# One row of small products per token tile, transposes apart, and a written order for TensorE in the last stage of a linear-attention kernel

## The chip, the cores and the metric

The kernel runs on one core of a Trainium2 chip. The core has five engines, each with its own queue of instructions that it works off in order: TensorE (PE in the profile; its weight loads are PEld), VectorE (DVE), ScalarE (ACT), GpSimd (POOL) and SyncE (SP), which here issues the transfers. [...] TensorE writes into PSUM, a small memory that DVE and ACT empty into the main on-chip memory, SBUF; transfers move data between SBUF and the memory outside (HBM). The metric is the device time of one execution in microseconds (us), the median of several runs.

## The reference

The input x has 2048 tokens of 1024 numbers. Two branches read its normalized form:

```python
xn = _layernorm(x)
# branch A: linear attention, 32 heads of 32
q, k, v = split(xn @ wqkv)
phi_q = concat([softmax(q @ w_phi), softmax(-(q @ w_phi))])     # per head, 64 features
phi_k = the same of k
kv = einsum("sf,sd->fd", phi_k, v);  z = sum_s phi_k            # per head
o  = (phi_q @ kv) / (phi_q @ z + 1e-6)
s  = o @ wo
# branch B: gated feed-forward, 1024 -> 3584 -> 1024
g  = silu( (silu(xn @ w1) * (xn @ w3)) @ w2 )
out = x + s * g
```

All numbers are 32-bit floats. The large products are made of three passes over a number split in a high and a low part.

## The kernel before

The kernel goes through stages: normalization, keys and values, the feed-forward branch, and last the queries with the attention output. The large products of the earlier stages are done by a Strassen-like scheme of seven products in place of eight; those stages are the same in both kernels. What the change touches is the last stage, which goes through the 16 token tiles of 128 tokens each.

For one token tile the last stage does this:

- `load_q` brings the tile of xn, `split_q` splits it into high and low parts (`xh`; a cast on ACT, line 92, and a subtraction on DVE, line 93).
- `project_q(xT, c)` makes half c of the tile's queries, already multiplied by w_phi: `project`, line 101, 24 matmuls of 128x128 by 512 columns, into a PSUM tile `pm` (tag "mm", three buffers).
- `queries(p, c)` turns that half into normalized features `e`: maxima, minima and two subtractions on DVE (lines 1000 to 1003), Exp on ACT (1006), a product with z, `ez`, on POOL (1007), two sums (1011 over e, 1015 over ez), a chain of small operations (1013 to 1020) and the last multiply (1021) on DVE.
- `attend(c, e)` is the small work on TensorE: e is transposed in two quarters of four 128x128 blocks (line 1146, PSUM tile `pt2`, three buffers), each copied to SBUF by ACT (`et`, line 1148), and multiplied by the per-head kv matrices `kvu` (line 1152): products with 64 rows and 32 columns of weights and 128 moving columns, 16 for each half, into the PSUM tile `po` of two banks, one buffer. A cast and a subtraction (`split`) make `oT` of it, high and low.
- `finish(i, oT)` multiplies oT by wo in two halves of 24 matmuls (`project`), multiplies by the gate g and adds x (`gx`), and stores.

The loop is skewed by one tile: while the queries of tile i are made, the features of tile i-1 are attended and finished. The first tile's features, `es[0]` and `es[1]`, are made at the end of the stage before: es[1] while the last but one round of that stage runs, es[0] in the last one.

The order of instructions on each engine is set by a scheduler that ranks by program order and its own cost model, wherever the program does not say otherwise. `in_order(engines)` opens a stretch in which the named engines keep the written order exactly; `in_order()` ends it. Before, the last stage has SP alone in written order, and only for the first iteration; TensorE's order is the scheduler's. It put the second row of small products, which needs `po` free again, among the matmuls of `project_q(xT, 1)`, and two of the second half's transposes ahead of the first row.

Of the kernel before, what the change touches and what calls it, by code (L numbers as in the profile page):

```python
# [8 lines left out]
F = mybir.dt.float32  # L9
# [8 lines left out]
P = 128  # L18
NT = S // P
# [10 lines left out]
def tile_kernel(ctx: ExitStack, tc: tile.TileContext, x, wkT, wqT, wv, wphi, wo, w1, w3, w2, out):  # L30
    nc = tc.nc
    open_pools = {}

    def pool(name, bufs, **kw):

        open_pools[name] = tc.tile_pool(name=name, bufs=bufs, reuse_waits="tile", **kw)
        return open_pools[name].__enter__()
# [5 lines left out]
    ENG = mybir.EngineType  # L43
# [3 lines left out]
    def in_order(*engines):  # L47

        if ordered:
            ordered.pop().__exit__(None, None, None)  # L50
        if engines:
            ordered.append(tc.manual_schedule(engines=set(engines)))
            ordered[0].__enter__()
# [18 lines left out]
    g_d = [dram.tile([P, D], F, name=f"g_d{i}") for i in range(NT)]  # L72
# [17 lines left out]
    def split(hi, lo, src, by=None):  # L90

        nc.scalar.copy(hi, src)  # L92
        (by or nc.vector).tensor_sub(lo, src, hi.bitcast(F))  # L93

    def project(ps, xT, w, tag="mm"):

        p = ps.tile([P, 512], F, name="pm", tag=tag, bufs=3 if tag == "mm" else BANKS["a"])
        n = 0
        for dch in range(ND):
            for a, b in PASSES:  # L100
                nc.tensor.matmul(p, xT[dch][:, a], w(dch, b), start=n == 0, stop=n == 3 * ND - 1)  # L101
                n += 1
        return p
# [34 lines left out]
    work = pool("work", 5)  # L138
# [5 lines left out]
    ps = pool("ps2", 2, space=PSUM)  # L144
# [25 lines left out]
    def quad(name, dt=R):  # L170
        return qp.tile([P, 2, 4, P], dt, name=name, tag="q")
# [7 lines left out]
    ident = misc.tile([P, P], F, name="ident")  # L179
# [134 lines left out]
    for j in range(4):  # L314
        sl = slice(32 * j, 32 * j + 32)
# [599 lines left out]
    ps = pool("ps", 2, space=PSUM)  # L915
    BANKS = {"a": 2, "b": 3, "c": 2}
    pend = None
    ready = []
    for c in range(2):
# [4 lines left out]
        for i in range(len(pairs)):  # L924
            nxt, end = {}, i + 1 == len(pairs)

            def steps():
                for j in range(7):
                    if j == 0:
                        if i + 2 == len(pairs) and c == 0:  # L930
                            for m in range(2):
                                wbn.update(fetch(3, m))
                        if not (end and c):
                            nxt.update(reload((i + 1) % len(pairs)))
                        if c and 0 < i < 5:
                            load_b(0, i - 1)

                    if end and c == 0 and j in (0, 1, 4, 5, 6):
                        wbn.update(fetch(3, {0: 2, 1: 3}.get(j, j)))
                    if end and c and j in (1, 4):  # L940
                        ready.append(a_first(0, 0) if j == 1 else a_second(*ready[0]))
                    yield

            pend = heads(i, xo, wb, steps(), pend)
# [5 lines left out]
    accp = pool("acc", 1)  # L950
# [13 lines left out]
    wq, wos, es = {}, {}, {}  # L964
# [15 lines left out]
    def load_q(i):  # L980
        two = quad("xf", F)
        for hf in range(2):
            nc.sync.dma_start(two[:, hf], xn_d[:, 4 * hf:4 * hf + 4, i * P:(i + 1) * P])
        return [two[:, hf] for hf in range(2)]

    def split_q(xf):
        xT = []
        for t in xf:
            xh = quad("xh")
            split(xh[:, 0], xh[:, 1], t)  # L990
            xT += [xh[:, :, k] for k in range(4)]
        return xT

    def queries(p, c):

        e = accp.tile([P, 16, 2, DH], F, name="e", tag="accE", bufs=3)
        ez = accp.tile([P, 2 * 512], F, name="ez", tag="accZ", bufs=3)
        mm = small.tile([P, 2, 16], F, name="mm2")
        p3 = p.rearrange("p (h f) -> p h f", f=DH)
        nc.vector.tensor_reduce(mm[:, 0, :], p3, axis=AX.X, op=OP.max)  # L1000
        nc.vector.tensor_reduce(mm[:, 1, :], p3, axis=AX.X, op=OP.min)
        nc.vector.tensor_sub(e[:, :, 0], p3, mm[:, 0, :].unsqueeze(2).to_broadcast([P, 16, DH]))
        nc.vector.tensor_sub(e[:, :, 1], mm[:, 1, :].unsqueeze(2).to_broadcast([P, 16, DH]), p3)
        ef = e.rearrange("p h s f -> p (h s f)")
        e3 = e.rearrange("p h s f -> p (h s) f")
        nc.scalar.activation(ef, ef, AF.Exp)
        nc.gpsimd.tensor_mul(ez, ef, zb[c])
        sums = small.tile([P, 2, 16, 2], F, name="sums")
        by = small.tile([P, 16, 2], F, name="by")
        t = small.tile([P, 2, 16], F, name="rho")  # L1010
        nc.vector.tensor_reduce(sums[:, 0].rearrange("p h s -> p (h s)"), e3, axis=AX.X, op=OP.add)

        nc.vector.reciprocal(t[:, 0], sums[:, 0, :, 1])
        nc.vector.tensor_mul(t[:, 0], sums[:, 0, :, 0], t[:, 0])
        nc.vector.tensor_reduce(sums[:, 1].rearrange("p h s -> p (h s)"), ez.rearrange("p (h f) -> p h f", f=DH),
                                axis=AX.X, op=OP.add)
        nc.vector.tensor_mul(t[:, 1], sums[:, 1, :, 1], t[:, 0])
        nc.vector.tensor_add(t[:, 1], t[:, 1], sums[:, 1, :, 0])
        nc.vector.reciprocal(by[:, :, 0], t[:, 1])
        nc.vector.tensor_mul(by[:, :, 1], by[:, :, 0], t[:, 0])  # L1020
        nc.vector.tensor_mul(e3, e3, by.rearrange("p h s -> p (h s)").unsqueeze(2).to_broadcast([P, H, DH]))
        return ef

    def project_q(xT, c, tag="mm"):
        return project(ps, xT, lambda k, a: wq[c, k][:, a], tag)
# [31 lines left out]
    for r, new in enumerate(steps):  # L1057
        kb, i = new or (NKB, 0)
# [5 lines left out]
        if new is None:  # L1064
            in_order(ENG.SP, ENG.Activation, ENG.DVE, ENG.Pool)
            xT = split_q(xf)
# [33 lines left out]
        if end:  # L1100
# [12 lines left out]
            if i == 4:  # L1113
                xf = load_q(0)
            elif i == 5:
                xT = split_q(xf)
            elif i > 5:
                if i == 6:

                    kvu = work.tile([P, 2, G, DH], F, name="kvu", tag="h1", bufs=2)  # L1120
                    for a in range(2):
                        for h in range(2):
                            sl = slice(64 * a + 32 * h, 64 * a + 32 * h + 32)
# [3 lines left out]
            if i == 7:  # L1127
                xf = load_q(1)
# [4 lines left out]
    ps = pool("ps4", 3, space=PSUM)  # L1133
    gate(*pairs[-1])
    for k in range(14, 16):
        load_wo(k, accp.tile([P, 2, 512], R, name="wos", tag="accW", bufs=2))
    in_order(ENG.SP)

    def attend(c, e):


        po = ps.tile([P, 2, 512], F, name="po", tag="po", bufs=1)
        for q in range(2):
            pt = ps.tile([P, 4, P], F, name="pt2", tag="tr", bufs=3)
            for g in range(4):
                nc.tensor.transpose(pt[:, g, :], e[:, (4 * q + g) * P:(4 * q + g + 1) * P], ident)  # L1146
            et = work.tile([P, 4, P], F, name="et", tag="w")
            nc.scalar.copy(et, pt)
            for g in range(4):
                for hh in range(2):  # L1150
                    sl = slice(64 * hh, 64 * hh + 64)
                    nc.tensor.matmul(po[32 * g:32 * g + 32, hh, q * P:(q + 1) * P], kvu[sl, g % 2, 4 * c + 2 * q + g // 2], et[sl, g],  # L1152
                                     start=True, stop=True, skip_group_check=True)
        oT = quad("oT")
        o4 = oT.rearrange("p u (h q) t -> p u h q t", q=2)
        split(o4[:, 0], o4[:, 1], po[:, :, :2 * P].rearrange("p h (q t) -> p h q t", t=P))
        return oT

    def finish(i, oT):
        for c in range(2):  # L1160
            cs = slice(c * 512, c * 512 + 512)
            gx = accp.tile([P, 2, 512], F, name="gx", tag="accZ", bufs=3)
            nc.sync.dma_start(gx[:, 0], g_d[i][:, cs])
            nc.sync.dma_start(gx[:, 1], x[i * P:(i + 1) * P, cs])
            p = project(ps, [t[:, :, k] for t in oT for k in range(4)], lambda k, a: wos[c, k][:, a])
            nc.vector.tensor_mul(gx[:, 0], p, gx[:, 0])
            (nc.vector if i + 1 == NT else nc.gpsimd).tensor_add(gx[:, 0], gx[:, 0], gx[:, 1])
            nc.sync.dma_start(out[i * P:(i + 1) * P, cs], gx[:, 0])

    pend = 0, es[0], es[1]  # L1170
    for i in range(1, NT):
        if i < NT - 1:
            xf = load_q(i + 1)
        e0 = queries(project_q(xT, 0), 0)
        oT = [attend(0, pend[1]), attend(1, pend[2])]
        p = project_q(xT, 1)
        if i + 1 < NT:
            xT = split_q(xf)
        e1 = queries(p, 1)
        finish(pend[0], oT)  # L1180
        pend = (i, e0, e1)
        if i == 1:
            in_order()
    finish(pend[0], [attend(0, pend[1]), attend(1, pend[2])])
    close("ps4", "rb", "acc", "q", "work", "small", "misc", "ra", "rw", "edge_r", "edge_l")


# [36 lines left out]
```

## Time and profile before

| | |
|---|---|
| time, median of 3 runs | 2427.62 us (2425.49 to 2428.64) |
| the profiled execution | 2427.67 us, of which the profile's span is 2425.9 us |
| TensorE busy | 2394.2 us, 99% of the span |
| DVE, ACT, POOL busy | 73%, 36%, 8% |
| last stage | from about 2020 us to the end |

A profile line of the timeline gives the start in us from the span's start, the time from the first start to the last end, the engine, the line of the kernel, the operation, the tile written and those read, shapes, and the count of instructions in the group. In brackets stands the idle time just before, and what ended it. TensorE's instructions overlap, so the distance between the starts of two groups tells more than the duration of one. Rows of windows give, for each stretch, the busy time and count of PE, PEld, DVE, ACT and POOL, then the granted TensorE clock as a share of full speed, and the transfers. The small products appear twice in the profile for each one in the program.

### The profile page before, as it was taken

The numbers are of one execution on the slowest core, as the hardware profiler recorded it, in microseconds if no ns is written. First come the engines' busy times: TensorE is split into PE (matmuls) and PEld (weight loads), VectorE is DVE, ScalarE is ACT, GpSimd is POOL, SyncE is SP. The second block draws the span as 40 slices with busy tenths as digits, with TensorE's granted clock in tenths as the row PEclk, the third lists the DMA queues.
The fourth block names the chain that finished last, engine by engine and source line by source line (L and its number), as shares of the span: only waits on it lengthen the run. The fifth ranks groups of instructions, "written<-read, shape, count | busy, mean of one in ns | idle before, by whom it ended". The sixth has DMA issues, their size and how long they took to land.

```text
span 2425.9 us, 35682 instructions
## 1 busy us (share of the span) xinstructions
PE 2394.2 (99%) x13650; PEld 1965.1 (81%) x13650; DVE 1773.2 (73%) x2883; ACT 880.4 (36%) x1549; POOL 196.4 (8%) x162
## 2 busy tenths in 40 slices
PE   6999999999999999999999999999999999999999
PEld 5888888888888888888787888888888887777777
DVE  7877787875688878764565666678878777777775
ACT  5545454443355444442111114322222244222221
POOL 2000000000000000000000000011111112222322
PEclk9999999999999999999999999999999999999999
DMA  8456799997788886666958745442445476222222
GB/s 280 141 193 226 261 337 341 319 321 221 254 296 296 311 281 239 238 219 240 339 175 345 249 157 200 175 163 89 157 174 182 157 255 231 73 89 86 70 88 70
DMA packets 295274, 517.86 MB, mean 213 GB/s; under 512 B 19904, under 2 KB 168128, under 8 KB 293312
## 3 DMA queue, kind: packets, MB, share of 16 engines
q1 hardware_dynamic: 295104, 515.59, 61.6%
q8 instruction: 107, 1.75, 0.3%
q14 instruction: 63, 0.52, 0.1%
HBM read 329.65 MB, written 185.87 MB: 213 GB/s over the span
## 4 chain that ended last, share of the span: by engine, by line
PE 95%; DMA 1%; DVE 1%; ACT 1%; SPq 0%; issue 0%; ACTq 0%; DVEq 0%
PE bankb L613 24%; PE pm L101 14%; PE bankb L1038 13%; PE bankc L613 12%; PE bankb L806 7%; PE bankc L1038 6%; PE banka L613 6%; PE bankc L806 3%; PE banka L1038 3%; PE banka L806 2%; PE po L1152 1%; PE pw L250 1%; PE pkv L791 1%; PE pt L1146 1%; DMA op2T<-wkv_d0T 1%; PE pt L218 1%
## 5 line engine op out<-in xcount | busy, mean ns | idle before, releaser
L93 DVE TENSOR_TENSOR bo<-rw,bo 128x512 fp32r<-128x512 f32 x336 | 230.4, 688 | 158.7 <-ACT bo L92 156.0
L92 ACT CAST bo<-rw 128x512 fp32r<-128x512 f32 x336 | 206.3, 618 | 5.5 <-DMA xo_d1S<-xoS 3.4
L1038 PE MATMUL bankb<-bo,as 128*128 128x512 f32 x816 | 200.9, 389 | 0.0
L101 PE MATMUL pm<-wq,xh 128*128 128x512 f32 x768 | 185.8, 394 | 0.0
L1038 PEld LDWEIGHTS bankb<-bo,as 128*128 128x128 f32 x816 | 153.2, 188 | 31.8
L101 PEld LDWEIGHTS pm<-wq,xh 128*128 128x128 f32 x768 | 141.9, 188 | 31.7 <-issue 3.0
L613 PE MATMUL bankb<-op0S,bo 128*128 128x512 f32 x672 | 162.9, 391 | 0.9 <-ACT op0S L92 0.5
L613 PE MATMUL bankc<-op0S,bo 128*128 128x512 f32 x672 | 162.4, 391 | 0.0
L613 PE MATMUL bankc<-op1S,bo 128*128 128x512 f32 x672 | 161.2, 389 | 0.0
L613 PE MATMUL bankb<-op1S,bo 128*128 128x512 f32 x672 | 161.2, 389 | 0.0
L613 PE MATMUL bankb<-op0A,bo 128*128 128x512 f32 x672 | 159.7, 391 | 0.6 <-DVE bo L93 0.3
L613 PE MATMUL bankb<-op1A,bo 128*128 128x512 f32 x672 | 157.5, 389 | 0.1
L613 PEld LDWEIGHTS bankb<-op1A,bo 128*128 128x128 f32 x672 | 126.0, 188 | 27.1 <-DVE u L655 0.9
L613 PEld LDWEIGHTS bankb<-op0S,bo 128*128 128x128 f32 x672 | 125.2, 188 | 27.5 <-ACT op0S L92 0.9
L613 PEld LDWEIGHTS bankb<-op1S,bo 128*128 128x128 f32 x672 | 126.1, 188 | 26.2
L613 PEld LDWEIGHTS bankc<-op1S,bo 128*128 128x128 f32 x672 | 126.1, 188 | 26.2
L613 PEld LDWEIGHTS bankb<-op0A,bo 128*128 128x128 f32 x672 | 125.1, 188 | 26.8 <-DVE bo L93 0.6
L613 PEld LDWEIGHTS bankc<-op0S,bo 128*128 128x128 f32 x672 | 125.3, 188 | 25.9 <-DVE op0S L93 0.3
L1038 PE MATMUL bankc<-bo,as 128*128 128x512 f32 x576 | 146.2, 389 | 0.0
L101 PE MATMUL pm<-wos,oT 128*128 128x512 f32 x576 | 136.2, 389 | 0.0
L101 PEld LDWEIGHTS pm<-wos,oT 128*128 128x128 f32 x576 | 108.0, 188 | 22.7 <-issue 0.2
L1038 PEld LDWEIGHTS bankc<-bo,as 128*128 128x128 f32 x576 | 108.1, 188 | 22.5
(234 smaller groups left out, 4249.3 us busy)
## 6 DMA issues: line engine op xcount, KB each, us to landing
rw<-in_w SPq DMA_DIRECT2D x112, 512.0 KB, 4.5
hr<-h_d SPq DMA_DIRECT2D x56, 512.0 KB, 3.5
h_d<-h SPq DMA_DIRECT2D x111, 256.0 KB, 5.1
xoS<-xo_d0S SPq DMA_DIRECT2D x32, 512.0 KB, 8.4
xoS<-xo_d1S SPq DMA_DIRECT2D x32, 512.0 KB, 3.6
room<-in_w SPq DMA_DIRECT2D x56, 256.0 KB, 5.9
xoA<-xo_d0A SPq DMA_DIRECT2D x24, 512.0 KB, 7.8
xoA<-xo_d1A SPq DMA_DIRECT2D x24, 512.0 KB, 3.6
```

The costliest lines, as they stand in the source:

```text
L92: nc.scalar.copy(hi, src)
L93: (by or nc.vector).tensor_sub(lo, src, hi.bitcast(F))
L101: nc.tensor.matmul(p, xT[dch][:, a], w(dch, b), start=n == 0, stop=n == 3 * ND - 1)
L218: nc.tensor.transpose(pt[:, k, :], half[:, k * P:(k + 1) * P], ident)
L250: nc.tensor.matmul(pw[:, g, :], wr[:, g], bd[:, 4 * c + g, :], start=True, stop=True)
L613: nc.tensor.matmul(bank[b], bos[tb, f][bn][:, w, k], ao[an][:, u, k], start=first and n == 0, stop=LAST[b] == an and n == 11, skip_group_c ...
L791: nc.tensor.matmul(pkv[sl, m], e[:, m // 4, (m % 4) * P + 32 * h:(m % 4) * P + 32 * h + 32], v[:, 4 * (m % 4) + h], start=first and m == 0 ...
L806: nc.tensor.matmul(bank[b], xo[an][:, u, k], wb[bn][:, w, k], start=an in ("A11", "A12", "S1") and n == 0, stop=LAST[b] == an and n == 11, ...
L1038: nc.tensor.matmul(bank[b], t[:, u, pos + k], bos[kb, bn, k][:, w], start=first and n == 0, stop=LAST[b] == an and n == 5, skip_group_chec ...
L1146: nc.tensor.transpose(pt[:, g, :], e[:, (4 * q + g) * P:(4 * q + g + 1) * P], ident)
L1152: nc.tensor.matmul(po[32 * g:32 * g + 32, hh, q * P:(q + 1) * P], kvu[sl, g % 2, 4 * c + 2 * q + g // 2], et[sl, g], start=True, stop=True ...
```

## The change

Three things are changed in the last stage.

- `turn_e` does the transposes and copies of one quarter of a feature half; `attend` takes four such copies and issues all 32 small products in one row, into one `po` tile of [128, 2, 4, 128], the same two banks with both halves side by side. The casts and subtractions for both halves of oT follow it.
- `finish` does one of its two halves, c, at a time. The transposes of the first half of the next features (`e0`) stand between the two halves; those of the second half (`e1`) stand right ahead of the row of small products. For the first tile, the transposes of `es[0]` stand ahead of the loop.
- TensorE is in written order in the whole of the last stage, with SP beside it until the end of the first iteration.

The written order on TensorE in one iteration is so: the first query projection, eight transposes, 32 small products, the second query projection, half of the output projection, eight transposes, the other half. In the built program the other engines' order moves too: on DVE the first subtraction into oT now stands behind the sum over ez and the reciprocal (before: ahead of the sum over e), the second one four small operations later; on ACT the two casts into oT stand together behind the Exp, and the copies of the transposes of e0 behind the Exp of e1. The number of instructions of each kind is the same.

```diff
-    in_order(ENG.SP)
-
-    def attend(c, e):
-        po = ps.tile([P, 2, 512], F, name="po", tag="po", bufs=1)
-        for q in range(2):
-            pt = ps.tile([P, 4, P], F, name="pt2", tag="tr", bufs=3)
-            for g in range(4):
-                nc.tensor.transpose(pt[:, g, :], e[:, (4 * q + g) * P:(4 * q + g + 1) * P], ident)
-            et = work.tile([P, 4, P], F, name="et", tag="w")
-            nc.scalar.copy(et, pt)
+    in_order(ENG.SP, ENG.PE)
+
+    def turn_e(e, q):
+        pt = ps.tile([P, 4, P], F, name="pt2", tag="tr", bufs=3)
+        for g in range(4):
+            nc.tensor.transpose(pt[:, g, :], e[:, (4 * q + g) * P:(4 * q + g + 1) * P], ident)
+        et = work.tile([P, 4, P], F, name="et", tag="w")
+        nc.scalar.copy(et, pt)
+        return et
+
+    def attend(ets):
+        po = ps.tile([P, 2, 4, P], F, name="po", tag="po", bufs=1)
+        for k, et in enumerate(ets):
             for g in range(4):
                 for hh in range(2):
                     sl = slice(64 * hh, 64 * hh + 64)
-                    nc.tensor.matmul(po[32 * g:32 * g + 32, hh, q * P:(q + 1) * P], kvu[sl, g % 2, 4 * c + 2 * q + g // 2], et[sl, g],
+                    nc.tensor.matmul(po[32 * g:32 * g + 32, hh, k], kvu[sl, g % 2, 2 * k + g // 2], et[sl, g],
                                      start=True, stop=True, skip_group_check=True)
-        oT = quad("oT")
-        o4 = oT.rearrange("p u (h q) t -> p u h q t", q=2)
-        split(o4[:, 0], o4[:, 1], po[:, :, :2 * P].rearrange("p h (q t) -> p h q t", t=P))
+        oT = []
+        for c in range(2):
+            o = quad("oT")
+            o4 = o.rearrange("p u (h q) t -> p u h q t", q=2)
+            split(o4[:, 0], o4[:, 1], po[:, :, 2 * c:2 * c + 2])
+            oT.append(o)
         return oT
...
-    def finish(i, oT):
-        for c in range(2):
-            cs = slice(c * 512, c * 512 + 512)
+    def finish(i, oT, c):
+        cs = slice(c * 512, c * 512 + 512)
...
-    pend = 0, es[0], es[1]
-    for i in range(1, NT):
+    ets, e1 = [turn_e(es[0], q) for q in range(2)], es[1]
+    for i in range(1, NT + 1):
         if i < NT - 1:
             xf = load_q(i + 1)
-        e0 = queries(project_q(xT, 0), 0)
-        oT = [attend(0, pend[1]), attend(1, pend[2])]
-        p = project_q(xT, 1)
-        if i + 1 < NT:
-            xT = split_q(xf)
-        e1 = queries(p, 1)
-        finish(pend[0], oT)
-        pend = (i, e0, e1)
+        if i < NT:
+            e0 = queries(project_q(xT, 0), 0)
+        ets += [turn_e(e1, q) for q in range(2)]
+        oT = attend(ets)
+        if i < NT:
+            p = project_q(xT, 1)
+            if i + 1 < NT:
+                xT = split_q(xf)
+            e1 = queries(p, 1)
+        finish(i - 1, oT, 0)
+        if i < NT:
+            ets = [turn_e(e0, q) for q in range(2)]
+        finish(i - 1, oT, 1)
         if i == 1:
-            in_order()
-    finish(pend[0], [attend(0, pend[1]), attend(1, pend[2])])
+            in_order(ENG.PE)
+    in_order()
```

More of the change, by code (lines that the diff above doesn't have):

```diff
@@ L1157, in attend @@
-        return oT
-    def finish(i, oT):
-        for c in range(2):
-            cs = slice(c * 512, c * 512 + 512)
[L1162 to L1168, printed above, removed]
@@ L1170, in tile_kernel @@
-    pend = 0, es[0], es[1]
-    for i in range(1, NT):
+        oT = []
[4 more added lines that the diff above has]
+            oT.append(o)
+        return oT
+    def finish(i, oT, c):
+        cs = slice(c * 512, c * 512 + 512)
+        gx = accp.tile([P, 2, 512], F, name="gx", tag="accZ", bufs=3)
+        nc.sync.dma_start(gx[:, 0], g_d[i][:, cs])
+        nc.sync.dma_start(gx[:, 1], x[i * P:(i + 1) * P, cs])
+        p = project(ps, [t[:, :, k] for t in oT for k in range(4)], lambda k, a: wos[c, k][:, a])
+        nc.vector.tensor_mul(gx[:, 0], p, gx[:, 0])
+        (nc.vector if i + 1 == NT else nc.gpsimd).tensor_add(gx[:, 0], gx[:, 0], gx[:, 1])
+        nc.sync.dma_start(out[i * P:(i + 1) * P, cs], gx[:, 0])
```

## The prediction

> **What bounds the kernel.** I read the page's engine table first, then PE's timeline of one token tile, then the other engines around it, then both ends of the last stage.
>
> ```profile
> PE 2394.2 (99%) x13650; PEld 1965.1 (81%) x13650; DVE 1773.2 (73%) x2883; ACT 880.4 (36%) x1549; POOL 196.4 (8%) x162
> ```
>
> TensorE is busy 99% of the span, so time goes only where PE works less, and comes only where PE waits. The stage the change touches runs from about 2020 us to the end. One token tile of it, PE's timeline (start, us, then the group):
>
> ```profile
> 2154.41 1.25 PE L1146 MATMUL pt<-ident,e 128*128 128x128 f32 x10
> 2155.74 0.94 PE L1152 MATMUL po<-et,kvu 64*32 64x128 f32 x32
> 2156.61 0.88 PE L1146 MATMUL pt<-ident,e 128*128 128x128 f32 x6
> 2157.24 1.84 PE L101 MATMUL pm<-wq,xh 128*128 128x512 f32 x7
> 2159.02 0.78 PE L1152 MATMUL po<-et,kvu 64*32 64x128 f32 x32
> 2159.72 4.19 PE L101 MATMUL pm<-wq,xh 128*128 128x512 f32 x17
> 2163.75 5.60 PE L101 MATMUL pm<-wos,oT 128*128 128x512 f32 x24
> ```
>
> I call the two query projections P0 and P1, the two output projections F0 and F1 (24 matmuls each), the transposes T and the small products S (each of the kernel's 32 is two instructions here, so 64). t0 is the moment a tile's P0 has issued; here 2154.41. From starts of groups: ten T take 1.33 up to S, six take 0.63 (0.105 each); S in two halves takes 0.87 and 0.70; the seven matmuls before the second S take 1.78 and the 17 after it 4.03. No wait of PE is printed in this tile. The start of the stage and later starts of T:
>
> ```profile
> 2020.23 5.60 PE L101 MATMUL pm<-wq,xh 128*128 128x512 f32 x24
> 2025.67 1.25 PE L1146 MATMUL pt<-ident,e 128*128 128x128 f32 x10
> ...
> 2077.45 1.25 PE L1146 MATMUL pt<-ident,e 128*128 128x128 f32 x10
> ...
> 2385.41 1.25 PE L1146 MATMUL pt<-ident,e 128*128 128x128 f32 x10
> ```
>
> P0's 24 matmuls take 2025.67 - 2020.23 = 5.44, 0.227 each; so the seven and the 17 above took 0.19 and 0.17 more than their number asks for, and a change between wide and small products costs about that each time, four times a tile. The starts of T are t0 of tiles 1, 3 and 15: the first two periods together are 51.78, the other twelve 307.96 / 12 = 25.66 each. 96 wide matmuls are 21.77 of that; 3.89 are T, S and changes.
>
> **The change: steady tiles.** Removed: one of the two small rows' entries and exits. 16 T stay at 0.109 = 1.74. One row of 64: entered at 0.24 (1.33 - 10 x 0.109), body and exit 0.70 plus two more sixteens at 0.33 (half of the 0.65 that a 32 would add), 1.35; re-entry of the wide ones 0.17. Sum 3.50 against 3.89: 0.39 less, period 25.27. Bounds for the row: twice 0.70 (no saving inside) and 2 x 0.50 + 0.20 = 1.20; I take the middle, since both halves show the same spacing. Now the covers in written order, with DVE and ACT of the same tile:
>
> ```profile
> 2155.10 1.07 ACT L1148 COPY et<-pt 128x512 f32<-128x512 f32 x2 [11.20 <-PE pt L1146]
> 2154.61 0.69 DVE L1000 TENSOR_REDUCE mm<-pm 128x16 f32<-128x512 f32 x1 [2.40 <-PE pm L101]
> ...
> 2165.94 0.68 DVE L1000 TENSOR_REDUCE mm<-pm 128x16 f32<-128x512 f32 x1
> ...
> 2173.42 0.63 DVE L1166 TENSOR_TENSOR gx<-pm,gx 128x512 f32<-128x512 f32 x1
> ...
> 2395.99 0.68 DVE L1000 TENSOR_REDUCE mm<-pm 128x16 f32<-128x512 f32 x1
> ...
> 2406.10 1.22 DVE L1021 TENSOR_TENSOR e<-e,by 128x1024 f32<-128x1024 f32 x1
> ```
>
> The row's first 32 instructions use copies made in the tile before; the last 32 need copies of T issued just ahead. Those copies end at t0 + 0.69 + 0.59 and + 1.76, and S reaches them at about t0 + 1.76 and 2.06: covered by S itself, without reserve to speak of; if ACT were late, PE waits as long. The copies of the other half (mid-F) queue behind the second Exp on ACT, but are needed only after t0 of the next tile, over 8 us on.
>
> The new wait is at F0. One PSUM tile means that the casts and the subtractions into oT come after all of S, and in the new DVE order the first oT subtraction stands behind the sum over ez, where before it stood ahead of the sum over e. The second query chain of this tile shows the length of that queue undisturbed: from its first reduce (2165.94) to the instruction behind the reciprocal (2173.42) 7.48, which itself takes 0.63. The first chain starts at t0 + 0.20, so oT's low half is ready at t0 + 8.31, and PE starts 0.15 to 0.2 later: 8.50. PE comes there by its own work at 0.87 (eight T) + 0.24 + 1.35 + 0.17 + 5.44 = 8.07, and the first matmul with the low half is the third, 8.52. The two are level. If PE's part were shorter than reckoned, DVE's 8.50 would hold and nothing more would be won, so 0.39 a tile is also about the most; if the queue is longer by x, each tile is longer by x. DVE's work has room: the second chain starts at 11.53 before, and some 0.7 later after, since subtractions that lay in a wait now lie ahead of it; from its start to the writing of e it takes 11.33 (2395.99 to 2407.32), and one multiply more ends it at about t0 + 24.2, below 25.27. The first e is written about 0.6 ahead of the second chain's start, 11.6, and T asks for it at t0 + 13.5. SP's loads of gx and xf stand behind the stores that wait for POOL's add, and shift with it by about 1 us against several us until they are used. These I cost at nothing.
>
> The first two tiles differ:
>
> ```profile
> 2045.56 0.63 DVE L1166 TENSOR_TENSOR gx<-pm,gx 128x512 f32<-128x512 f32 x1
> ...
> 2051.55 0.69 DVE L1166 TENSOR_TENSOR gx<-pm,gx 128x512 f32<-128x512 f32 x1 [2.14 <-PE pm L101]
> ```
>
> In the first iteration SP is in written order, the second gx is loaded after the first out is stored, and 5.99 us lie between the two multiplies (the page blames PE; what came last there was the load). This is unchanged, so the first chain of tile 2 starts 0.8 late, and where oT and F0 are level F0 now waits for it. I take 0.15 of gain for tiles 1 and 2 together. Tiles 1 to 14: -0.15 - 12 x 0.39 = -4.83.
>
> **The change: the start.** In written order the first instructions of the stage are the eight T of es[0], and PE can issue nothing past them; before, P0 of tile 1 went first and hid them. es[0] is the last thing that the stage before made:
>
> ```profile
> 2023.75 1.23 DVE L1021 TENSOR_TENSOR e<-e,by 128x1024 f32<-128x1024 f32 x1
> ```
>
> It is written at 2024.98. DVE's order ahead of it is the same in both kernels, and the PE work it hangs on was issued by 2020.23. PE needs about 0.15 behind such a write (2406.10 + 1.22 to the row of 2407.47, below): T starts at 2025.13, P0 at 2026.00, and t0 of tile 1 is 2031.44 instead of 2025.67: +5.77, of which 4.9 is an idle PE. Queued behind T are P0, all of tile 1, and with it every engine.
>
> A PE that idles for 4.9 us may come back slow. What this trace shows:
>
> ```profile
> 14.55 3.75 PE L250 MATMUL pw<-bd,room_b 128*128 128x128 f32 x16 [14.55 <-DMA room_b<-in_wkT]
> 18.10 4.58 PE L218 MATMUL pt<-ident,xt 128*128 128x128 f32 x28
> 24.59 0.66 PE L218 MATMUL pt<-ident,xt 128*128 128x128 f32 x4 [1.90 <-ACT xf L223]
> ...
> 31.51 1.95 PE L250 MATMUL pw<-bd,room_b 128*128 128x128 f32 x16
> ...
> 2420.30:2423.70 3.40, 0.94 (x5) 0.44 (x3) 1.38 (x2) 0.00 (x0) 0.00 (x0) 1.00 0.02 8
> 2423.70:2425.90 2.20, 0.00 (x0) 0.00 (x0) 0.00 (x0) 0.00 (x0) 0.00 (x0) 0.50 0.28 106
> ```
>
> After 14.55 us of nothing, sixteen products took 3.75 us, later 1.95: half speed. The 28 transposes behind them took 4.58 where 0.109 each would be 3.2 with the last one's end; some 13 of them were slow too, so half speed lasted about 6.2 us into the work. After 1.9 us of idle four transposes took the normal time. At the end the granted clock is 0.50 some 2.5 us after the last matmul (2418.36 + 2.88). So 4.9 us idle is past the point. 6.2 us at half speed lose 0.47 of it, 2.9, on the one restart in the trace; ends 0 (no drop) and 3.3 (7 us); I take 2.5, nearest to the restart, a little under it because PE works densely from the first.
>
> [...]
>
> **The change: the end.**
>
> ```profile
> 2407.47 0.41 PE L1146 MATMUL pt<-ident,e 128*128 128x128 f32 x2 [0.80 <-ACT et L1148]
> ...
> 2408.59 0.59 ACT L92 CAST oT<-po 128x512 fp32r<-128x512 f32 x1 [1.19 <-PE po L1152]
> 2418.36 2.88 PE L101 MATMUL pm<-wos,oT 128*128 128x512 f32 x12
> ```
>
> Before, PE's last issue slot ends at 2418.36 + 12 x 0.227 = 2421.08, t0 + 35.67 of tile 15. After, F1 ends at about t0 + 19.8, and the last T needs the second e of tile 15: its chain started at t0 + 10.58 before, starts 0.5 later behind two oT subtractions, and lasts 11.33: T at t0 + 22.55, after 2.7 of idle. Then po is done 0.87 + 0.24 + 1.43 = 2.54 later (0.78 for a row of 32, 0.65 for 32 more), the cast follows by 0.1 (an estimate) and takes 0.59, F0 starts at + 3.3 and its third matmul, behind the subtraction, at + 4.04; 46 wide ones are 10.43: end at t0 + 37.0. That is +1.3. Here the cover of S's results is gone (no P1 is left), while before half of them lay under F0's first matmuls. 2.7 us of idle lie between the 1.9 that did nothing and the 4.9; whether the clock halves again is open, at the price of the start. I take 1.5, half of 2.9; ends 0 and 3.3.
>
> **Sum.** +5.77 + 2.5 - 4.83 + 1.3 + 1.5 = +6.2. The profiled execution took 2427.67 (its span 2425.9 and 1.8 around it), the median of the runs 2427.62, so nothing is to be moved: 2433.8, +0.25%. A measurement of this kernel can tell about 0.2%, 4.9 us, from no change.
>
> **Rivals.** (1) The clock drops at the start alone: 2433.8 - 1.5 = 2432.3, about on the bound of 0.2%. For it: 2.7 us is short. (2) It drops nowhere: 2.5 less again, 2429.8. For it: the row at 24.59; against it the 0.50 at the end. (3) The first T does not wait, because es[0] is written before PE gets there; then T only moves, start term +0.87, no first drop, 2427.67 + 0.87 - 4.83 + 1.3 = 2425.0, or up to 2428 with a drop at the end: not slower. It decides if e is written before 2020.2; the row at 2023.75 is against it. (4) DVE's queue ahead of oT grows by 0.3 us or more a tile (POOL's product late, ACT's Exp behind a copy): 14 x 0.3 = 4.2 more, 2438. Nothing in the rows shows such a delay, but PE in written order would meet every one. (5) The one row saves nothing, small products costing by number alone: 4.8 more, 2438.6; the 0.17 to 0.24 per change speak against it.
>
> **Numbers.** Forecast 0.42, (1) 0.25, (2) 0.12, (3) 0.06, (4) and (5) together 0.15. The range reaches from (2) to (4): 2429 to 2438.5. The forecast's own range, with the clock terms' ends, is 2431.5 to 2436. Slower by over 0.2%: nine tenths of the forecast, half of (1), all of (4) and (5), 0.65; faster by over 0.2% only if (3) comes with a larger gain per tile, 0.04; the rest 0.31.
>
> **What would show it.** On PE's timeline: an idle of 4.9 before the first transposes of the stage, put down to DVE's e, and groups of 128x128 at double spacing behind it, with a granted clock under 1.0 in that slice; periods of 25.2 to 25.3 in tiles 3 to 14, one row of 64 small products; small waits at the third matmul of F0 on DVE's oT; 2.7 of idle before the last eight transposes. Wrong would be: no idle at 2020, or periods above 25.5 or below 25.1.

## The result, and the profile after

| | before | changed |
|---|---|---|
| time, median | 2427.42 us (2425.49 to 2429.3, 11 runs) | 2433.46 us (2432.37 to 2434.9, 11 runs) |
| the profiled execution's span | 2425.9 us | 2432.5 us |

The ratio is 1.0026, 95% interval 1.0017 to 1.0035: slower by 6.0 us, where 2433.8 was forecast. Both profiles have nearly the same busy time of TensorE (2394.2 and 2395.2 us); the difference is waiting and clock. The start of the last stage, from the timeline of TensorE of the changed kernel, with DVE's line for the features that it waits for (start, us, engine, line, operation, tiles, shapes, count, and in brackets the idle before and what ended it):

```profile
2018.68 1.52 PE L1038 MATMUL bankb<-bo,as 128*128 128x512 f32 x6
2023.56 1.23 DVE L1021 TENSOR_TENSOR e<-e,by 128x1024 f32<-128x1024 f32 x1
2024.93 1.94 PE L1144 MATMUL pt<-ident,e 128*128 128x128 f32 x8 [4.73 <-DVE e L1021]
2026.53 7.27 PE L101 MATMUL pm<-wq,xh 128*128 128x512 f32 x24
2033.64 1.03 PE L1144 MATMUL pt<-ident,e 128*128 128x128 f32 x8
2034.60 1.30 PE L1155 MATMUL po<-et,kvu 64*32 64x128 f32 x64
2035.84 5.73 PE L101 MATMUL pm<-wq,xh 128*128 128x512 f32 x24
2041.41 0.62 PE L101 MATMUL pm<-wos,oT 128*128 128x512 f32 x2
2043.22 5.29 PE L101 MATMUL pm<-wos,oT 128*128 128x512 f32 x22 [1.20 <-DVE oT L93]
```

TensorE stands for 4.73 us until DVE has written the features of the first tile. What comes then is slow: eight transposes in 1.94 us where the next eight take 1.03, and 24 wide matmuls in 7.27 where 5.6 is usual. The views of windows show the granted clock (the number before the last two):

```profile
2024.40:2027.70 3.30, 2.77 (x11) 2.61 (x12) 0.39 (x1) 1.17 (x2) 0.00 (x0) 0.50 1.01 376
...
2031.20:2034.50 3.30, 3.30 (x20) 2.73 (x18) 0.66 (x2) 0.17 (x1) 0.00 (x0) 1.00 0.94 274
...
2412.00:2416.00 4.00, 3.65 (x72) 2.88 (x72) 0.41 (x1) 1.40 (x3) 1.27 (x1) 0.57 0.73 235
```

By the trace's record of the granted clock it is halved from 2022.98 to 2029.80 us, that is 2.0 us before the first wait ends and for 4.87 us of the work behind it, and once more near the end, from 2412.10 to 2415.51. A steady tile and the end, TensorE's timeline again, with DVE's first subtraction into oT in the steady tile:

```profile
2085.97 1.04 PE L1144 MATMUL pt<-ident,e 128*128 128x128 f32 x8
2086.94 1.30 PE L1155 MATMUL po<-et,kvu 64*32 64x128 f32 x64
2088.18 5.73 PE L101 MATMUL pm<-wq,xh 128*128 128x512 f32 x24
2093.68 0.63 DVE L93 TENSOR_TENSOR oT<-po,oT 128x512 fp32r<-128x512 f32 x1
2093.75 5.90 PE L101 MATMUL pm<-wos,oT 128*128 128x512 f32 x24
2099.49 1.03 PE L1144 MATMUL pt<-ident,e 128*128 128x128 f32 x8
...
2389.55 1.04 PE L1144 MATMUL pt<-ident,e 128*128 128x128 f32 x8
...
2406.68 2.88 PE L101 MATMUL pm<-wos,oT 128*128 128x512 f32 x12
2411.96 1.82 PE L1144 MATMUL pt<-ident,e 128*128 128x128 f32 x8 [2.40 <-DVE e L1021]
2413.71 1.95 PE L1155 MATMUL po<-et,kvu 64*32 64x128 f32 x64
2416.41 6.01 PE L101 MATMUL pm<-wos,oT 128*128 128x512 f32 x24 [0.76 <-ACT oT L92]
...
2424.97 2.88 PE L101 MATMUL pm<-wos,oT 128*128 128x512 f32 x12
```

From tile 3 (2085.97) to tile 15 (2389.55) a period is 303.58 / 12 = 25.30 us, 0.36 less than before. All 64 small products stand in one row, as written. The first output projection takes 2099.49 - 2093.75 = 5.74 from start to the next start where 24 matmuls without a wait take 5.44: it waits 0.30 for that subtraction. The whole, by the marks of the prediction (the starts of the transposes in tiles 1, 3 and 15):

| stretch | before | changed | difference |
|---|---|---|---|
| to the first transposes of tile 1 | 2025.67 | 2033.64 | +7.97 |
| tiles 1 and 2 | 51.78 | 52.33 | +0.55 |
| tiles 3 to 14 | 307.96 | 303.58 | -4.38 |
| tile 15 to TensorE's last issue (last group + 12 x 0.227) | 35.67 | 38.14 | +2.47 |

The sum is +6.61, the difference of the two spans.

### The profile page after: what moved, and what is told of

The parts are those of the page before. It is cut to its first block, busy times and chain, and to the rows that moved or that the text cites. A ratio compares the mean times of both kernels' runs of the same rounds, so it can differ in the third digit from the quotient of the medians.

```text
span 2432.5 us, 35683 instructions
## 1 busy us (share of the span) xinstructions
PE 2395.2 (98%) x13650; PEld 1971.2 (81%) x13650; DVE 1772.6 (73%) x2883; ACT 880.1 (36%) x1549; POOL 196.5 (8%) x162
```

## The experiments

Each kernel ran beside the kernel before on the same chip. "Time" is the median; the ratio is to the kernel before. The runs e1 to e4, e5 to e8, and e9 with e10 form three groups, in which the kernel before took 2426.63, 2427.17 and 2427.01 us (2427.42 beside the changed kernel). So a difference between runs of two groups is uncertain by nearly 1 us, and where it matters it is also given against the kernel before of the same group.

| run | time, us | ratio, 95% interval |
|---|---|---|
| e1, first transposes behind the first projection | 2425.96 | 0.9996 (0.9988 to 1.0005) |
| e2, last tile in halves | 2432.61 | 1.0024 (1.0014 to 1.0034) |
| e3, both | 2424.51 | 0.9991 (0.9983 to 1.0) |
| e4, both, and the oT subtraction earlier | 2419.42 | 0.9968 (0.9956 to 0.9981) |
| e5, the first wait filled with work | 2430.75 | 1.0015 (1.0006 to 1.0023) |
| e6, both waits filled | 2430.38 | 1.0012 (1.0004 to 1.0021) |
| e7, the kernel before in written order | 2576.85 | 1.0615 (1.06 to 1.0629) |
| e8, as e4 with two rows of small products | 2425.37 | 0.9992 (0.9983 to 1.0001) |
| e9, one row, the scheduler's order | 2428.0 | 1.0005 (0.9996 to 1.0014) |
| e10, as e4 without the last tile in halves | 2418.86 | 0.9966 (0.9954 to 0.9979) |

The theory: the start costs a wait and a halved clock, the end the same on a smaller scale, and the tiles gain up to a ceiling set by DVE's queue. The first rival: the loss is spread over the stage by the written order. The second: the written order, not the one row, brings the gain.

**e1: the place of the first transposes.**

```diff
-    ets, e1 = [turn_e(es[0], q) for q in range(2)], es[1]
+    ets, e1 = None, es[1]
     for i in range(1, NT + 1):
...
             e0 = queries(project_q(xT, 0), 0)
+        if i == 1:
+            ets = [turn_e(es[0], q) for q in range(2)]
```

> The changed kernel with one thing moved: the eight transposes of es[0] stand behind the first query projection of the stage, directly ahead of those of es[1], where before they stood ahead of it. Theory (the start costs 4.7 us of idle TensorE and about 2.5 us of half clock, and the tiles gain): the first row of small products starts about 7.3 us earlier, no idle of more than 1 us near 2020, time about 2426.2, tile periods unchanged at 25.30. Rival (the loss is spread over the stage by the written order, and the wait at the start only shifts work that would wait elsewhere): time stays at 2432 to 2434.

2425.96 us, 7.5 less than the changed kernel (6.7 against the kernel before of each). TensorE's timeline of this run:

```profile
2018.80 5.61 PE L101 MATMUL pm<-wq,xh 128*128 128x512 f32 x24
2024.25 1.93 PE L1144 MATMUL pt<-ident,e 128*128 128x128 f32 x16
```

No wait is left ahead of the transposes; the projection covers the time until the features are there. From the end of the stage before (2020.04 in the changed kernel, 2018.80 here) to the first row of small products it is 14.56 us in the changed kernel and 7.31 here (that row starts at 2026.11), 7.3 less as expected. So the start's term is shown, with its size, and the rival of a spread loss falls.

**e2 and e3: the last tile in halves.**

```diff
+    p = bank()
+    part(p, oT[0], 1, 0)
+    po = ps.tile([P, 2, 4, P], F, name="po", tag="po", bufs=1)
+    o = half(po, 0, ets)
+    part(p, oT[1], 1, 1)
...
+    for c in range(2):
+        part(ends[c], o, c, 0)
+    ets = [turn_e(e1, q) for q in range(2)]
+    o = half(po, 1, ets)
+    for c in range(2):
+        part(ends[c], o, c, 1)
```

`half` issues 32 of the small products and makes one half of oT; `part` issues the 12 output matmuls that need that half.

> The changed kernel with another last tile: the small products of its first half go between the two halves of the last but one tile's second output projection, the output products that need only this half come next, and the transposes of the second half, its small products and the rest of the output products come last. Theory (the end costs 2.4 us, by an idle of 2.4 us before the last transposes, the half clock behind it and 0.8 us before the last output products): about 2431.1, no wait above 2 us in the last 40 us, granted clock 1.0 there until the last matmul. Rival (the end is bound by the second feature chain on DVE whatever TensorE does): 2433, the same as the changed kernel.

> Both edits together, the start and the end. Theory (three independent terms): 2433.5 - 7.3 - 2.4 = 2423.8, 0.15% faster than the kernel before the change, and what is left is the gain of the tiles. Rival (the terms are not independent, tile 1 and tile 2 give the start back by their waits at the first output projection): 2426 or more.

e2 came out at 2432.61, 0.9 below the changed kernel where 2.4 was expected; against the kernel before of each, both are 6.0 slower, so no gain of e2 alone is shown. e3 came out at 2424.51, 1.5 below e1 of the same group. In e2's timeline the end is this:

```profile
2407.55 3.47 PE L1209 MATMUL pm<-wos,oT 128*128 128x512 f32 x14
2412.65 2.58 PE L1209 MATMUL pm<-wos,oT 128*128 128x512 f32 x10 [1.63 <-DVE oT L93]
2415.07 2.89 PE L1209 MATMUL pm<-late,oT 128*128 128x512 f32 x12
```

The wait before the last transposes is gone, and a new one of 1.63 us stands before the first half's output: its oT subtraction is queued on DVE behind the second feature chain. The start's gain is kept when the end is changed too, so the rival of e3 falls, but the end was mended only in part; e10 says more on it.

**e4 and e10: the oT subtraction earlier on DVE.**

```diff
-            e0 = queries(project_q(xT, 0), 0)
+            pm0 = project_q(xT, 0)
...
         oT = attend(ets)
+        if i < NT:
+            e0 = queries(pm0, 0)
```

TensorE's written order stays the same; on DVE the scheduler now puts the first oT subtraction between the two sums.

> As the run with both edits, and the features of a tile's first half are traced behind its small products, so that on DVE the first subtraction into oT comes ahead of the sum over ez. Theory (in steady tiles the first output projection waits 0.27 us for that subtraction, at the end of DVE's queue): the wait goes, period about 25.03, 14 tiles give 3.8 us, time about 2420. Rival (the wait is TensorE's own restart after the change of shape, or DVE gives the same time back elsewhere): period stays at 25.3, time 2423.8.

2419.42 us, 5.1 below e3, where 3.8 was expected. Its timelines, TensorE and then DVE:

```profile
2077.74 1.04 PE L1144 MATMUL pt<-ident,e 128*128 128x128 f32 x8
2078.70 1.30 PE L1155 MATMUL po<-et,kvu 64*32 64x128 f32 x64
2079.94 5.73 PE L101 MATMUL pm<-wq,xh 128*128 128x512 f32 x24
2085.51 5.61 PE L101 MATMUL pm<-wos,oT 128*128 128x512 f32 x24
2090.95 1.03 PE L1144 MATMUL pt<-ident,e 128*128 128x128 f32 x8
```

```profile
2081.61 1.22 DVE L1011 TENSOR_REDUCE sums<-e 128x32 f32<-128x1024 f32 x1 [1.19 <-ACT e L1006]
2082.74 0.68 DVE L93 TENSOR_TENSOR oT<-po,oT 128x512 fp32r<-128x512 f32 x1
```

The output projection is down to 2090.95 - 2085.51 = 5.44. In the changed kernel the subtraction came 7.71 us after the tile's first transposes (2093.68 against 2085.97), here 5.00. So the wait was DVE's queue, not a restart of TensorE. The waits of 1.20 and 0.53 in tiles 1 and 2 are gone too (in e1, where only the first transposes moved, 0.28 and 0.4 were left). e10 is this kernel with the last tile left as in the change:

> The fastest run so far without its other last tile, so that what the last tile's split brings is measured there: the first transposes behind the first projection, the subtraction into oT ahead of the sum over ez, the last tile as in the changed kernel. Theory (the split of the last tile brings 1.2 us by TensorE's timeline, and up to 3 more in executions where the clock would halve in the last wait): 2420.6 to 2423. Rival (the split brings nothing): 2419.4.

2418.86 us: not slower than e4, and below the 2420.6 to 2423 of the theory. So the halves bring nothing once the rest is mended: from the first transposes of tile 15 to TensorE's last issue the profile of e4 has 36.4 us and that of e10 36.2, since the halves have a wait on oT of their own (1.44 us in e4). Its median is the lowest of all, 0.34% below the kernel before.

**e5 and e6: work in the waits.** Matmuls whose result nobody reads stand ahead of the first transposes (16), and in e6 ahead of the last (10) too.

```diff
+    idle = ps.tile([P, 512], F, name="idle", tag="mm", bufs=3)
+    for n in range(16):
+        nc.tensor.matmul(idle, xT[n // 2][:, 0], wq[0, n // 2][:, n % 2], start=n == 0, stop=n == 15)
     ets, e1 = [turn_e(es[0], q) for q in range(2)], es[1]
```

> The changed kernel with 16 matmuls of 512 columns added ahead of the first transposes of the last stage; nothing reads their result. They fill 3.6 us of the 4.7 us in which TensorE waits there. Theory (beside the wait, the idle halves the granted clock, and this alone costs 2.5 us): the wait for the features stays and ends at the same moment, but the transposes and the query projection behind it run at full speed, 7.9 us to the next transposes' start falls to 6.3, time about 2431.0. Rival (the first products of the stage are slow for another reason, or the clock does not depend on the idle): 2433.5 or above.

> The same, and 10 such matmuls ahead of the last transposes too, in the 2.4 us wait of the last tile. Theory: the half clock over the last transposes and small products (1.82 and 1.95 us where 1.03 and 1.30 are usual) goes as well, 1.5 us, time about 2429.5, granted clock 1.0 from 2020 on. What then remains of the loss is waiting alone. Rival (the last products are slow because their operands are late): no change against the run with the start filled alone, 2431.

```profile
2019.64 3.79 PE L1177 MATMUL idle<-wq,xh 128*128 128x512 f32 x16
2024.51 1.06 PE L1144 MATMUL pt<-ident,e 128*128 128x128 f32 x8 [1.08 <-DVE e L1021]
2025.33 5.72 PE L101 MATMUL pm<-wq,xh 128*128 128x512 f32 x24
2030.89 1.03 PE L1144 MATMUL pt<-ident,e 128*128 128x128 f32 x8
```

In e5 the transposes wait for the same e, but run in 1.06 us and the projection in 5.72; from the transposes' start to the next ones it is 6.38 instead of 8.71, 2.3 less. The time is 2430.75, 2.7 less (2.5 against the kernel before of each). So here the idle itself halves the clock, and this is about 2.5 of the 8 us at the start. e6 is 0.4 below e5, within the scatter: no gain is shown. A reason stands in e5's own timeline, where nothing was done about the end:

```profile
2409.57 1.06 PE L1144 MATMUL pt<-ident,e 128*128 128x128 f32 x8 [2.40 <-DVE e L1021]
2410.57 1.30 PE L1155 MATMUL po<-et,kvu 64*32 64x128 f32 x64
```

The same wait of 2.40 us, and no slow products behind it. A wait of this length was followed by slow products in some of the profiles and not in others: the small products behind it took 1.95 and 1.96 us in the changed kernel and e1, after 2.40 us each, but 1.30 or 1.31 in e5, e9 and e10, after 2.40, 2.43 and 2.21. What the record of the clock shows of this stands under What the hardware showed.

**e7: the written order alone.** The kernel before, with `in_order(ENG.SP, ENG.PE)` in place of `in_order(ENG.SP)`, `in_order(ENG.PE)` after the first iteration, and nothing else.

> The kernel before with TensorE in its written order in the whole last stage, and nothing else: four transposes, their copy, 16 small products, four times a tile in turn. Theory (the gain per tile comes from one row with its transposes apart, and a written order alone makes TensorE wait for every copy and for the PSUM tile): at least 2.5 us more per tile, four waits for ACT's copies in each, 2465 or more. Rival (the written order is what saves the time per tile): periods of 25.3 or less, 2422 to 2428.

2576.85 us, 6.2% slower. One tile of it:

```profile
2168.99 0.45 PE L1152 MATMUL po<-et,kvu 64*32 64x128 f32 x16 [0.68 <-ACT et L1148]
2169.37 0.66 PE L1146 MATMUL pt<-ident,e 128*128 128x128 f32 x4
2170.76 0.45 PE L1152 MATMUL po<-et,kvu 64*32 64x128 f32 x16 [0.73 <-ACT et L1148]
2171.14 0.66 PE L1146 MATMUL pt<-ident,e 128*128 128x128 f32 x4
2176.25 0.68 PE L1152 MATMUL po<-et,kvu 64*32 64x128 f32 x16 [4.46 <-DVE rho L1014]
2176.87 1.11 PE L1146 MATMUL pt<-ident,e 128*128 128x128 f32 x4
```

Rows wait for their copies, the third for po to be read by DVE (the line names `rho`; the subtraction that reads po stands behind the sum over ez on DVE and ends at 2176.11), and behind that wait the clock is down (1.11 for four transposes, 0.66 ahead of it; the granted clock from 2150 to 2180 us is 0.92). Over the whole stage TensorE waits 34 us for copies and 68 us in the third rows, so of the two the wait for po costs more. The second rival falls: a written order is a loss where the order written has the dependent work next to its source. What the changed order gains comes from the one row and the transposes apart from it; e9 below has the same period without the written order.

**e8: one change of shape.** e4 with the row cut in two by seven matmuls of the second projection.

```diff
+        row(po, ets[:2], 0)
+        p = ps.tile([P, 512], F, name="pm", tag="mm", bufs=3)
+        query_part(p, xT, 0, 7)
+        row(po, ets[2:], 2)
```

> The fastest run so far (start, end and the earlier oT subtraction) with the small products in two rows of 32 with seven matmuls of the second query projection between them, all else alike. It prices one change of shape. Theory (a second entry and exit cost 0.17 + 0.19 us and this stands on TensorE's path in each of 15 tiles): period 0.3 to 0.4 longer, 25.35, time about 2424.5. Rival (the row's own products are what cost, changes of shape cost nothing): 2419.4, the same as that run.

```profile
2105.26 0.67 PE L1180 MATMUL po<-et,kvu 64*32 64x128 f32 x32
2105.86 1.89 PE L1195 MATMUL pm<-wq,xh 128*128 128x512 f32 x7
2107.68 0.67 PE L1180 MATMUL po<-et,kvu 64*32 64x128 f32 x32
2108.28 4.15 PE L1195 MATMUL pm<-wq,xh 128*128 128x512 f32 x17
2112.27 5.64 PE L101 MATMUL pm<-wos,oT 128*128 128x512 f32 x24
```

2425.37 us against 2419.42. Rows and the second projection take 2112.27 - 2105.26 = 7.01, in e4 2085.51 - 2078.70 = 6.81: a second entry and exit cost 0.20 a tile, less than the 0.3 to 0.4 expected. 15 x 0.20 = 3.0 of the 5.9 us are explained by this. The two profiles, whose spans differ by 6.3, show the rest: tiles 1 and 2 take 1.3 us more, with new waits for oT at the output projection (0.42 in tile 2), tiles 3 to 14 take 2.7 more (a period of 25.21 against 24.99), and the last tile 2.4 more, with a wait of 1.97 for oT in place of 1.44 and, right behind it, ten matmuls that take 2408.80 - 2404.82 = 3.98 us to the next group's start, where those of e2 take 2415.07 - 2412.65 = 2.42.

**e9: one row without the written order.** `in_order(ENG.SP)` and no order for TensorE after it.

> The changed kernel without the written order on TensorE: its order is the scheduler's. In the steady tiles this is the same order; at the start the scheduler puts the first transposes behind ten matmuls of the first query projection. Theory (the loss is the place of the first transposes and the end, not the one row): the wait at the start falls from 4.7 to about 2.5 us with at most a short half clock, periods stay at 25.30, time about 2429 (2428 without any half clock at the start, 2430.5 with it). Rival (one row costs by itself): 2433.

```profile
2021.78 2.43 PE L101 MATMUL pm<-wq,xh 128*128 128x512 f32 x10
2026.67 1.07 PE L1144 MATMUL pt<-ident,e 128*128 128x128 f32 x8 [2.46 <-DVE e L1021]
```

2428.0 us, the same as the kernel before, 5.5 below the changed one. The scheduler puts ten matmuls ahead of the first transposes; the wait is 2.46 in place of 4.73, and in this profile nothing behind it is slow (at the end of the changed kernel a wait of 2.40 was followed by the half clock). In the steady tiles its order is the written one, with the same period of 25.30, and its end from tile 15's first transposes is 36.5 us, against 36.8 in e5, whose end has no half clock either. So the change's loss over this is, but for the clock at the end, the written place of eight transposes, once in the kernel.

## Why the prediction was right

The total was right within 0.4 us, its terms less closely. The tiles gained 1.0 us less than forecast (3.83 against 4.83), and the two ends cost 0.6 less in the profile (10.44 against 11.07); that the total is so near is luck in part. The mechanism, a wait and a half clock at the start and the end against a gain per tile, is the one that the runs show.

- **The start: +5.77 and 2.5 for the clock.** Measured +7.97 in the profile, with the stage begun 0.19 earlier, so 8.2 against 8.3. The idle is 4.73 (4.9 forecast), and filling it took 2.3 off by the timeline and about 2.5 by the medians. Right in mechanism and size: the row of e that it was read from starts at 2023.56 us in the changed kernel, 2023.75 before. The clock's 2.5 was drawn from one restart with 6.2 us at half speed, cut down to 2.5 by the reason that PE works densely; in the changed kernel the half clock began 1.95 us ahead of the work and lasted 4.87 us into it, 2.4 us of loss (see What the hardware showed). So the size of this term was met; that dense work shortens the half clock was the author's guess, and no run shows it.
- **Tiles 3 to 14: 0.39 each.** Measured 0.36. The two ways to the output projection were called level; they are not. The transposes with the change to the row take 0.97, not 1.11, the row up to the next wide matmul 1.24, not 1.35, and the projection behind it 5.57, not 5.61, so TensorE is there at t0 + 7.78, 0.29 earlier than forecast, and waits for DVE. What saved the number is the ceiling that the prediction drew from DVE's queue: the oT subtraction starts at t0 + 7.71 (7.68 forecast). The term that failed is the size of TensorE's own part; the gain it would have given is seen in e4, a period of 24.99 (2377.66 - 2077.74 over 12), 0.67 below the kernel before.
- **Tiles 1 and 2: -0.15.** Measured +0.55, the one term of wrong sign. The prediction has no term for the load of ACT's function table ahead of the first Exp. In the changed kernel it starts only when Exp's input is written (at 2036.32 us, after 0.98 us in which ACT stood idle) and so stands whole on the chain: it takes 1.28 us, the first oT subtraction comes at t0 + 8.90 where steady tiles have 7.71, and TensorE waits 1.20 for oT. The kernel before has the same load there, but its first subtraction stood ahead of the sum over e, so the output projection did not wait. A table load need not start so late: the one at 2011.73 us, in the stage before, ran while the input of its Exp was still being made, and Exp then waited 3.54 us for it. The late gx, which the prediction counted, made the 0.53 of tile 2.

```profile
2036.38 1.28 ACT L1006 ACT_TABLE_LOAD   x1 [0.98 <-issue]
2037.68 1.06 ACT L1006 ACTIVATE e<-e 128x1024 f32<-128x1024 f32 x1
```

- **The end: +1.3, and 1.5 for the clock.** Measured +2.47 in the profile that has the half clock. e5, without it, has 2421.19 + 2.72 - 2387.16 = 36.75 (its last group and its tile 15's first transposes, from its timeline), +1.1. So the wait is 1.1 and the clock, where it drops, 1.4. The forecast's 1.5 was the middle between a drop and none, so that it meets the price of a drop is luck. That it drops only in some executions was the open point of rival (1). The 0.1 that the cast was to follow by, an estimate, is 0.11: the small products end at 2415.66 and the cast starts at 2415.77.
- **Rivals.** (1), a drop at the start alone, stays possible for some executions: the one in the profile has both drops, but e5's end shows that the wait of 2.40 need not halve the clock. (2), no drop anywhere, falls by the half clock behind the first wait; e6, which fills both waits, shows what it would have given: 2430.4, against 2429.8 forecast for it. (3), no wait at the start, falls by the row with 4.73; e1, which has no such wait, gives 2426.0, against 2425.0 forecast for it. (4) falls, as the oT subtraction comes 0.03 later than forecast and not 0.3, and (5) falls: the period is 25.30, and e8 shows that changes of shape do cost, 0.20 for one more pair.

## What to carry to other kernels

Before an order is written out, the first round needs its own look: work that is covered in the steady state (here transposes between two projections) has no cover where the pipeline starts and ends, and an engine in written order stands still there (TensorE for 4.73 us at the start of this stage). One moved line was worth 6.7 to 7.5 us, more than the 3.8 that the 14 tiles gained. When one engine's work per round is shortened, the next ceiling is read from the other engines' queues, and a change of trace order on those (e4, 5.1 us) can give as much again: e10 is 0.34% faster than the kernel before, where the change by itself was 0.26% slower.

## What the hardware showed

- The trace of the changed kernel records three stretches at half clock between stretches at full clock: from 1155.99 us for 3.41 us, from 2022.98 for 6.83 (twice 3.41) and from 2412.10 for 3.41. The second lasts 4.87 us into the work behind its wait, the third 3.55. Their starts lie 866.99 and 389.12 us apart, 254 and 114 times a step of 3.413. If the trace is divided into steps of this length from these starts, the steps right ahead of the three have 1.83, 2.77 and 2.40 us without a running matmul (the ends of matmuls are modelled in the profile, so the sums are close and not exact). Of the other steps at full clock, from 19.35 us on, where the record begins, to the end of the last matmul, none has more than 1.31. Of the steps at half clock, one with 1.96 us without a matmul was followed by another, and three with none by full clock. The kernel before, divided in the same way from its one recorded drop at 2423.71 us, has 2.47 us in the step ahead of it and at most 1.46 (from 20.73 us) in the others since its record begins, at 20.73. The wait of 2.40 us in the changed kernel lay whole within one step; how the equal wait in e5 lay, behind which the products were not slow (1.06 and 1.30 us for the two groups), is not shown. An estimate from these numbers: a wait of 4.73 us has at least 2.37 us in one such step wherever the steps begin, more than the 1.83, so it would halve the clock each time.
- Two short stops in the middle of the kernel, outside the change, were enough for the first of the three: waits of 0.88 and 1.44 us, of which 1.83 us (0.39 and 1.44) lie in the step ahead of 1155.99, with the half clock of 3.41 us behind them. In the kernel before the waits there are 0.88 and 1.29, and the recorded clock stays at 1.0. The half clock cost little: from the start of the small products between the two waits to the start of the third group behind them it is 9.38 us in the changed kernel and 8.99 in the kernel before, where TensorE, at full clock, waits 1.04 us more for a load.
- ACT's second cast from po waits for DVE's subtraction from the other half of the same tile (4.05 us of idle before it in the profile's last full tile), although the halves do not overlap; what holds it back was not tried. The cast is needed only by the second half of each output projection's products, and no wait of TensorE for it is printed in the steady tiles.
